# Second layer of a fused attention and two-layer kernel: the output product of two batches as seven block products in place of eight, with w_out streamed

## The chip, the cores and the metric

The kernel runs on one core of one Trainium2 chip. The metric is the time of one execution in device microseconds. TensorE (PE) does the matmuls, VectorE (DVE), ScalarE (ACT) and GpSimd (POOL) the rest, and SyncE's queue (SP) issues most DMAs.

## The reference

Everything is float32 in the result; the weights come as 64-bit floats.

```python
# attention: x (8, 8, 512, 64), state (8, 8, 32, 64)
attn_out = concat([xread, sread], axis=2)          # 512 + 32 rows per batch
x = attn_out.transpose(0, 2, 1, 3).reshape(4352, 512)
x = ((x @ w1) * (x @ w2)) @ w3 @ w_out             # first layer, d_ff 1024
out = ((x @ wa) * (x @ wb)) @ wo2                  # second layer, d_ff 1536
```

The change concerns the last line: `h = (x @ wa) * (x @ wb)`, of 1536 columns, times `wo2`, 1536 x 512. `wo2` is called w_out here where no other is meant.

## The kernel before

Each float32 operand of a matmul is split into a high and a low fp32r part, and three products (high-high, high-low, low-high; `PASSES`) are added up in PSUM. SBUF is managed by hand as 47 tiles ("units") of 128 x 1024 words; a unit is taken and given back in program order, with an estimated time at which it is free. All instructions of a queue run in program order. The code also keeps an estimate of the time on each engine, by which small tasks are put between the matmuls.

The first layer takes 0 to 565 us. While it runs, the weights of the second layer come in: class `Intake` ("ab") loads a block f of 128 columns of wa and wb as 64-bit words, converts them (ACT, DVE, POOL), makes the sums S1 to S4 of the quarter blocks A11 to A22, splits all of it, and stores it to DRAM (`w_d`). As a "third" it also converts the 128 rows f of w_out, splits them and stores them to `z_d`. Blocks 0, 1, 2, 9, 10, 11 (`AB_AT`) do so in the first layer, blocks 3 to 8 (`AB_LATER`) while pair 0 of the second layer runs; these stay in SBUF until used.

The second layer runs over four pairs g of batches (`block2`), the two batches being the columns of one 2 x 2 block product. For each of the 12 blocks f, the two products x @ wa and x @ wb of both batches come as seven block products (Winograd's form, `product`, L1497) of 6 matmuls of 512 columns, which accumulate in three PSUM banks r, v and q; ACT and DVE combine them into e1, e2, e5 and from these the h block of batch 2g (e1, cast and split at once) and that of batch 2g+1 (product of e2 and e5 on POOL, kept in f32 as hb). The output product of batch 2g is put between the products of the next f (`accumulate`, L1509): 4 tiles of 128 rows x 3 passes, 12 matmuls of 512 columns. After the last f, the h blocks of batch 2g+1 are split one by one (`second_split`) and multiplied, 144 matmuls, together with the last 12 of batch 2g. All 12 blocks of split w_out stay in SBUF (z_t). The weights `w_d` are loaded two blocks ahead, four units per f, and the features of the next pair (class `Features`, tiles xB and x) are loaded, subtracted and split in the output stage.

The 256 rows of the states are done once in pair 0: `state_step` for each f (24 matmuls of 256 columns, L1552) and `state_output` (72 of 512 columns, L1581).

```python
for c, (m, q) in enumerate(PASSES):           # output(), L1507
    nc.tensor.matmul(t, lhsT=h[:, m, part * P : (part + 1) * P], rhs=z_t[f][:, q, :], ...)
```

Of the kernel before, what the change touches and what calls it, by code (L numbers as in the profile page):

```python
# [43 lines left out]
SPLIT_AHEAD = 2  # L44
# [6 lines left out]
START_BY = 3.0  # L51
# [8 lines left out]
def attention_moe_moe2(  # L60
# [142 lines left out]
    z_d = [dp.tile([P, 2, DM], F32R, name=f"z_d{f}") for f in range(NF2)]  # L203
    w_d = [dp.tile([P, 4, 1024], F32R, name=f"w_d{f}") for f in range(NF2)]
# [690 lines left out]
    class Intake:  # L895
# [3 lines left out]
        def __init__(self, name, pair, third, order):  # L899
            self.name, self.pair, self.third, self.order = name, pair, third, order  # L900
            self.count = len(order)
            self.next = 0
            self.tasks = []
            self.cols = {}
            self.rows = {}

        def start(self, tasks=2, reserve=0):
            if (
# [8 lines left out]
                if self.third is not None:  # L917
                    raws.append(load64(f"{self.name}t{f}_", self.third[f * P : (f + 1) * P, :]))
                    t = charge(D=1.45) + 2.0
# [3 lines left out]
        def stages(self, f, raws):  # L923
# [10 lines left out]
            def take_third():  # L934
                o["t"] = Convert(f"{name}t", raws[2:])
                o["t"].take(0)

# [9 lines left out]
            def sums():  # L947
                a21, a22, a11, a12 = (halves(o["c"].out)[:, i] for i in range(4))
# [18 lines left out]
            def store_part(i):  # L967
                for j, t in enumerate(o["p", i]):
                    nc.sync.dma_start(out=w_d[f][:, 2 * i + j].bitcast(F32), in_=t.bitcast(F32))
                if f in AB_AT:  # L970
                    free(*(f"w0_{f}_{2 * i + j}" for j in range(2)), at=until[0] + 2.5)
                else:
                    w_t.setdefault((0, f), []).extend(
                        t.rearrange("p (b k c) -> p b k c", b=4, k=2) for t in o["p", i]
                    )
                self.cols[f] = i == 1

            def split_third():
                z = o["z"] = flat(unit(f"z{f}", F32R), DM)
                split(z[:, 0, :], z[:, 1, :], o["t"].out)  # L980
                free(f"{name}t")

            def store_third():
                nc.sync.dma_start(out=z_d[f].bitcast(F32), in_=o["z"].bitcast(F32))
                if f in AB_AT:
                    free(f"z{f}", at=until[0] + 2.5)
                else:
                    z_t[f] = o["z"]
                self.rows[f] = True
# [6 lines left out]
            if self.third is None:  # L996
                out.append((2, {"A": 1.1, eng: {"G": 2.4, "V": 1.1}[eng]}, split_columns))
            else:
# [3 lines left out]
                    (0, dict(A=1.1), take_third),  # L1002
                    (1, {eng: {"G": 2.6, "V": 1.4}[eng]}, sums),
                    (2, work, lambda: split_part(0)),
                    (1, dict(V=0.6, G=1.2), lambda: o["t"].make()),
                    (0, dict(D=3.0), lambda: store_part(0)),
                    (2, work, lambda: split_part(1)),
                    (1, dict(A=0.6, V=0.6), split_third),
                    (0, dict(D=3.0), lambda: store_part(1)),
                    (0, dict(D=1.5), store_third),  # L1010
# [20 lines left out]
        def need(self, f):  # L1031
            while f in self.order and (
                not self.cols.get(f) or self.third is not None and f not in self.rows
            ):
                left = len(vacant), len(self.tasks), sum(len(t[1]) for t in self.tasks)
                self.start()
                self.run(0, force=True)
                if left == (len(vacant), len(self.tasks), sum(len(t[1]) for t in self.tasks)):
# [3 lines left out]
    z_t = {}  # L1042
    sw = Intake("sw", (w1, w2), None, list(range(NF1)))
    ab = Intake("ab", (wb, wa), wo2, [*AB_AT, *AB_LATER])
# [109 lines left out]
    A21, A22, A11, A12, S1, S2, S3, S4 = range(8)  # L1154
    NG = B // 2

    def load_w(g, f):
# [3 lines left out]
        ts = []  # L1161
        for i in range(4):
            t = unit(f"w{g}_{f}_{i}", F32R)
            nc.sync.dma_start(out=t.bitcast(F32), in_=w_d[f][:, i].bitcast(F32))
            ts.append(t.rearrange("p (b k c) -> p b k c", b=4, k=2))
        w_t[g, f] = ts

    def load_z(f):
        if f in AB_LATER:
            return  # L1170
        z_t[f] = flat(unit(f"z{f}", F32R), DM)
        nc.sync.dma_start(out=z_t[f].bitcast(F32), in_=z_d[f].bitcast(F32))

    def weights(g, f, block, k):
        return [w_t[g, f][2 * (block // 4) + m][:, block % 4, k, :] for m in range(2)]
# [225 lines left out]
    for b in range(B):  # L1401
# [9 lines left out]
        def fills1(f, b=b):  # L1411
            def middle():
                attend(MIDDLE, b, f)
                sw.run(HORIZON[0])
                ab.run(HORIZON[0])

            def behind():
# [20 lines left out]
                if NF1 * b + f >= SW_FROM:  # L1438
                    sw.start(SW_TASKS, reserve=1)
                if NF1 * b + f >= AB_AT.get(ab.order[min(ab.next, NF2 - 1)], NF1 * B):  # L1440
                    ab.start(2, reserve=AB_RESERVE)
                sw.run(HORIZON[0])
                ab.run(HORIZON[0])

# [17 lines left out]
    def fills_s(f):  # L1462
        def middle():
            sw.run(HORIZON[1])
            ab.run(HORIZON[1])
            if f > 0:
                xf[0].run(1, keep=8 if sw.next < NF1 else 4)

        def behind():
# [5 lines left out]
            ab.run(HORIZON[1])  # L1475
            xf[0].run(1, keep=8 if sw.next < NF1 else 4)
            if f >= NF1 - 3 and (0, 0) not in w_t and room(5):
# [29 lines left out]
    def output(t, h, f, part, first, last):  # L1507
        for c, (m, q) in enumerate(PASSES):
            nc.tensor.matmul(  # L1509
                t,  # L1510
                lhsT=h[:, m, part * P : (part + 1) * P],
                rhs=z_t[f][:, q, :],
                start=first and c == 0,
                stop=last and c == 2,
            )
        now[0] += 3 * 512 / 2400 * 1.0625

# [6 lines left out]
    def store(i, t, o, nxt):  # L1524
        dst = out[i * SB : i * SB + S, :].rearrange("(p t) e -> p t e", t=NT)
        if nxt:
            if t % 2:
# [255 lines left out]
```

## Time and profile before

| what | us |
|---|---|
| median of 3 runs (lowest, highest) | 1343.9 (1341.16, 1345.19) |
| the profiled execution | 1342.51 |
| its span, first to last instruction | 1340.7 |
| PE busy | 1300.3 |
| DVE, ACT, POOL busy | 612.0, 550.2, 439.3 |
| mean granted TensorE clock | 0.988 |

The span is what the trace covers; the execution takes 1.8 us more. Matmuls overlap in the trace, so the sum of their durations is larger than the time in which PE is busy.

### The profile page before, as it was taken

How to read it: one execution, taken by the hardware profiler on the slowest of the kernel's cores; microseconds unless marked ns; L12 is line 12 of the kernel's file. 1: busy time of each engine (PE TensorE's matmuls, PEld its weight loads, DVE VectorE, ACT ScalarE, POOL GpSimd, SP SyncE). 2: the span in 40 equal slices, each digit the busy share in tenths (PEclk: the TensorE clock that was granted, in tenths of full speed). 3: DMA queues.
4: the chain of work that ended last, by engine and by line, in shares of the span. 5: the costliest groups of instructions: out<-in, count | busy, mean ns of one | idle time of the engine just before them, and what ended most of it. 6: DMA issues, size and time to landing. Idle time of an engine off the chain costs nothing.

```text
span 1340.7 us, 17395 instructions
## 1 busy us (share of the span) xinstructions
PE 1300.3 (97%) x6596; PEld 1054.2 (79%) x6596; DVE 612.0 (46%) x792; ACT 550.2 (41%) x951; POOL 439.3 (33%) x352
## 2 busy tenths in 40 slices
PE   3998999999999999999999999999999999999998
PEld 1765768778777789888888888888888888888876
DVE  6676215646666667455532712232722326323240
ACT  7676455655565666354421412211422114221130
POOL 5554214454464477255510430110411103211100
PEclk6999999999999999999999999999999999999999
DMA  9977368493566552777373265542664434744301
GB/s 312 285 234 236 110 205 246 140 290 126 205 205 219 173 174 74 241 269 264 126 267 110 95 215 193 173 149 72 222 218 158 150 115 149 246 173 157 110 0 64
DMA packets 120662, 240.24 MB, mean 179 GB/s; under 512 B 44673, under 2 KB 65153, under 8 KB 120577
## 3 DMA queue, kind: packets, MB, share of 16 engines
q1 hardware_dynamic: 116000, 222.86, 50.5%
q0 software_dynamic: 4576, 16.26, 3.1%
q8 instruction: 52, 0.85, 0.2%
q14 instruction: 34, 0.27, 0.1%
HBM read 173.54 MB, written 65.54 MB: 178 GB/s over the span
## 4 chain that ended last, share of the span: by engine, by line
PE 89%; DMA 4%; DVE 3%; ACT 2%; issue 1%; POOL 1%; SPq 1%; ACTq 0%; POOLq 0%; DVEq 0%
PE r L1497 20%; PE o L1509 19%; PE v L1497 10%; PE x2p L1110 9%; PE bp L1051 5%; PE q L1497 5%; PE ap L1051 5%; PE abs L1552 3%; PE wp L358 2%; PE pb L315 2%; PE x2f L1291 2%; PE f L1051 1%; PE os L1581 1%; PE xt L388 1%; PE bs L1051 1%
## 5 line engine op out<-in xcount | busy, mean ns | idle before, releaser
L1509 PE MATMUL o<-z,h 128*128 128x512 f32 x1152 | 276.6, 389 | 1.3 <-ACT h L136 1.3
L1509 PEld LDWEIGHTS o<-z,h 128*128 128x128 f32 x1152 | 216.1, 188 | 47.0 <-ACT h L136 1.7
L1672 POOL TENSOR_TENSOR hb<-e,e 128x512 f32<-128x512 f32 x48 | 62.9, 1311 | 453.5 <-DVE e L1522 453.4
L136 ACT CAST h<-e 128x512 fp32r<-128x512 f32 x48 | 29.8, 621 | 364.8 <-DVE e L1675 350.8
L1110 PE MATMUL x2p<-hp,ws 128*128 128x512 f32 x672 | 161.9, 390 | 0.0
L1110 PEld LDWEIGHTS x2p<-hp,ws 128*128 128x128 f32 x672 | 125.8, 188 | 26.2
L142 POOL TENSOR_TENSOR pl<-pr,ph 128x512 fp32r<-128x512 f32 x64 | 83.1, 1320 | 120.6 <-ACT ph L136 74.0
L1522 DVE TENSOR_TENSOR e<-e,q 128x512 f32<-128x512 f32 x48 | 33.0, 688 | 195.7 <-PE q L1497 195.7
L1075 DVE TENSOR_TENSOR hfp<-asbp,bp 128x512 f32<-128x512 f32 x56 | 38.3, 684 | 93.6 <-PE bp L1051 89.9
L142 DVE TENSOR_TENSOR hp<-hfp,hp 128x512 fp32r<-128x512 f32 x56 | 54.1, 965 | 40.0 <-ACT hp L136 38.7
L1522 DVE TENSOR_TENSOR e<-e,v 128x512 f32<-128x512 f32 x48 | 33.0, 688 | 85.4 <-PE v L1497 85.4
L1497 PE MATMUL r<-xT2h,w 128*128 128x512 f32 x192 | 67.1, 390 | 0.0
L1497 PE MATMUL r<-xB11h,w 128*128 128x512 f32 x192 | 66.9, 389 | 0.0
L1497 PE MATMUL v<-xT1h,w 128*128 128x512 f32 x192 | 66.9, 389 | 0.0
L1497 PE MATMUL q<-xB21h,w 128*128 128x512 f32 x192 | 66.9, 389 | 0.0
L1497 PE MATMUL r<-xT3h,w 128*128 128x512 f32 x192 | 66.9, 389 | 0.0
L1497 PE MATMUL v<-xB22h,w 128*128 128x512 f32 x192 | 66.9, 389 | 0.0
L1497 PE MATMUL r<-xT4h,w 128*128 128x512 f32 x192 | 66.9, 389 | 0.0
L136 ACT CAST hp<-hfp 128x512 fp32r<-128x512 f32 x56 | 34.7, 620 | 57.0 <-DVE hfp L1075 52.2
L1069 ACT COPY asbp<-ap 128x512 f32<-128x512 f32 x56 | 33.1, 591 | 56.3 <-PE ap L1051 56.2
L142 DVE TENSOR_TENSOR h<-e,h 128x512 fp32r<-128x512 f32 x48 | 35.5, 739 | 33.4 <-ACT h L136 33.4
L1051 PE MATMUL bp<-ah,ph 128*128 128x512 f32 x112 | 47.9, 428 | 1.4 <-DVE a L473 0.9
(476 smaller groups left out, 2815.4 us busy)
## 6 DMA issues: line engine op xcount, KB each, us to landing
w<-w_d SPq DMA_DIRECT2D x168, 512.0 KB, 5.1
w_d<-w SPq DMA_DIRECT2D x48, 512.0 KB, 2.9
p_d<-sg SPq DMA_DIRECT2D x128, 128.0 KB, 2.5
pr<-p_d SPq DMA_DIRECT2D x32, 512.0 KB, 5.2
x<-in_x_dram SPq DMA_DIRECT2D x64, 128.0 KB, 4.6
sw<-in_moe_w_dram SPq DMA_DIRECT2D x16, 512.0 KB, 5.2
xB<-x_d SPq DMA_DIRECT2D x16, 512.0 KB, 4.8
x_d<-x2sp POOLq DMA_DIRECT2D x14, 512.0 KB, 5.8
```

The costliest lines, as they stand in the source:

```text
L136: nc.scalar.copy(hi, src)
L142: (eng or nc.vector).tensor_tensor(out=lo[:, i], in0=src[:, i], in1=hi[:, i].bitcast(F32), op=ALU.subtract)
L315: nc.tensor.matmul(t, lhsT=st_s[rows, (bg * NP + p) * P : (bg * NP + p + 1) * P], rhs=conv[f"wk{p}_{nh}"].out[rows, half[i]], start=True, ...
L1051: nc.tensor.matmul(dst[:, :n], lhsT=l[m], rhs=r[q], start=i == 0 and j == 0, stop=i == k - 1 and j == 2,)
L1069: nc.scalar.copy(a_sb[:, :n], pa[:, :n])
L1075: nc.vector.tensor_tensor(out=hf[:, :n], in0=a_sb[:, :n], in1=pb[:, :n], op=ALU.mult)
L1110: nc.tensor.matmul(acc[j], lhsT=w_s[f][:, m, j * P : (j + 1) * P], rhs=h[:, q, :n], start=per == 1 and f == 0 and i == 0, stop=f == NF1 - ...
L1497: nc.tensor.matmul(t, lhsT=w[m], rhs=xf[g].parts[x][q][:, k, :], start=first and k == 0 and i == 0, stop=k == 1 and i == 2, skip_group_che ...
L1509: nc.tensor.matmul(t, lhsT=h[:, m, part * P : (part + 1) * P], rhs=z_t[f][:, q, :], start=first and c == 0, stop=last and c == 2,)
L1522: nc.vector.tensor_tensor(out=out, in0=x, in1=y, op=ALU.add)
L1552: nc.tensor.matmul(t[:, w * 256 : (w + 1) * 256], lhsT=l[m], rhs=x_s[k][q], start=k == 0 and i == 0, stop=k == 3 and i == 2,)
L1672: nc.gpsimd.tensor_tensor(out=h2[-1][:, f % 2, :], in0=e2, in1=e5, op=ALU.mult)
```

## The change

Both batches of a pair are now the two columns of a second block product. The h blocks of both are kept in f32 for the whole pair: the rows of h in two halves (f under 6 and from 6 on) and two batches make the blocks 11, 12, 21, 22, each of three chunks (j) of 1024 columns (two f of 512). POOL makes the sums S1 to S4 of h, each chunk one operation. w_out's halves are combined likewise: class `IntakeZ` converts rows c and c+6 together, makes T1 to T4 and stores the seven split operands to `z_d[p]`. Six such tasks are started at set steps of the first layer (`Z_AT`) or, if they are late, in pair 0.

The output stage has 21 steps (7 products p, 3 chunks j). A step has 24 matmuls of 256 columns: 2 blocks, 4 tiles of 128 rows, 3 passes. The h operand is split three steps ahead, and the w_out operand (512 KB) is loaded from DRAM three steps ahead, for each pair anew; no part of w_out stays in SBUF. Results are copied or added to the output tiles from the banks after each product. The last pair does its last product in two halves of the rows. The states' rows go the same way, 18 matmuls of 256 columns after each product of pair 0. In the loop over f no output matmul remains; T4 of f is issued after the first two products of f+1; weight units are reloaded one by one as they come free, in a new order of blocks (`PLACES`), 3.5 units per f for pairs 1 to 3; a block of weights is stored by eight DMAs of 256 KB in place of four of 512 KB.

```diff
-SPLIT_AHEAD = 2
+Z_AT = {0: 17, 1: 23, 2: 29, 3: 35, 4: 41, 5: 44}
+LOOK = 3
+Z_LOOK = 3
+PLACES = (0, 2, 6, 7, 1, 3, 4, 5)
+TERMS = ("11", "12", "S2", "S1", "S3", "S4", "22")
+X_FROM = 7
+W_AT = {11: 0, 17: 1}
...
-    z_d = [dp.tile([P, 2, DM], F32R, name=f"z_d{f}") for f in range(NF2)]
-    w_d = [dp.tile([P, 4, 1024], F32R, name=f"w_d{f}") for f in range(NF2)]
+    z_d = [dp.tile([P, NF2 // 2, 2, DM // 2], F32R, name=f"z_d{p}") for p in range(7)]
+    w_d = [dp.tile([P, 8, 2, 256], F32R, name=f"w_d{f}") for f in range(NF2)]
...
-                    nc.sync.dma_start(out=w_d[f][:, 2 * i + j].bitcast(F32), in_=t.bitcast(F32))
+                    for n in range(2):
+                        a, b = PLACES[4 * i + 2 * n : 4 * i + 2 * n + 2]
+                        nc.sync.dma_start(
+                            out=w_d[f][:, a : b + 1 : b - a, j, :].bitcast(F32),
+                            in_=t.rearrange("p (h b c) -> p h b c", h=2, b=2)[:, n].bitcast(F32),
+                        )
...
+    class IntakeZ(Intake):
...
+            def sums():
+                b11, b12, b21, b22 = (o["c"].out[:, i * 256 : (i + 1) * 256] for i in range(4))
+                o["s"] = unit(f"zs{c}")
+                t2, t1, t3, t4 = (o["s"][:, i * 256 : (i + 1) * 256] for i in range(4))
+                for out, x, y in ((t1, b12, b11), (t2, b22, t1), (t3, b22, b12), (t4, b21, t2)):
+                    nc.vector.tensor_tensor(out=out, in0=x, in1=y, op=ALU.subtract)
...
+    class Output:
...
+        def combine(self, out, x, y, op, eng="G"):
+            ENGINES[eng].tensor_tensor(out=out, in0=x, in1=y, op=op)
...
+        def split(self, p, j):
+            term = TERMS[p]
+            names = [f"r{self.name}_{term}{q}{j}" for q in "hl"]
+            hi, lo = (unit(n, F32R)[:, : self.width] for n in names)
+            name, src = self.raw[term, j]
+            split(hi, lo, src)
...
+    def z_load(g, p, j):
+        name = f"zz{g}_{p}_{j}"
+        t = unit(name, F32R).rearrange("p (c q e) -> p c q e", c=2, q=2)
+        nc.sync.dma_start(out=t.bitcast(F32), in_=z_d[p][:, 2 * j : 2 * j + 2].bitcast(F32))
...
+    CHAIN = "rqrvrvr"
+    FIRST = (True, True, False, True, False, False, False)
...
-            if one is not None:
-                accumulate(one, f - 1, (0, 1))
...
+            h = [flat(out2.raw[f"{i + 1}{half}", j][1], S)[:, c, :] for i in range(2)]
+            nc.gpsimd.tensor_tensor(out=h[1], in0=e2, in1=e5, op=ALU.mult)
+            if f + 1 < NF2:
+                begin(f + 1)
             product(r, g, f, A22, "T4", False)
-            nc.vector.tensor_tensor(out=e1, in0=e1, in1=r, op=ALU.mult)
-            one = flat(unit(f"h{name}", F32R), S)
-            split(one[:, 0, :], one[:, 1, :], e1)
+            nc.vector.tensor_tensor(out=h[0], in0=e1, in1=r, op=ALU.mult)
+            reload(f, 3)
...
+            if half == 2 and c == 1:
+                out2.split(0, j)
+                out2.sum("S1", j)
+                out2.sum("S3", j)
...
+        for s, (p, j, tiles) in enumerate(steps):
+            n = s + LOOK
+            if n < 21:
+                out2.split(*order[n])
+            if s == 0:
+                out2.sum("S2", 2)
+            if 5 <= s < 8:
+                out2.sum("S4", s - 5)
+            if s + Z_LOOK < 21:
+                z_load(g, *order[s + Z_LOOK])
+            if not last_pair:
+                if s in W_AT:
+                    load_w(g + 1, W_AT[s])
+                if s >= X_FROM:
+                    xf[g + 1].run(2 if s % 2 else 1)
...
+            for k in range(2):
+                for i in tiles:
+                    dst = banks[c, i // 2][:, i % 2 * 256 : i % 2 * 256 + 256]
+                    for n, (m, q) in enumerate(PASSES):
+                        nc.tensor.matmul(
+                            dst,
+                            lhsT=hl[m][:, k, i * P : (i + 1) * P],
+                            rhs=z[:, k, q, :],
...
+            if j == 2:
+                if g == 0:
+                    state_part(p)
+                evacuate(p, sorted({i // 2 for i in tiles}))
```

## Rows read from the trace of the kernel before

**Rows 1.** The page: busy time by engine; the chain that ended last, by engine.

```profile
PE 1300.3 (97%) x6596; PEld 1054.2 (79%) x6596; DVE 612.0 (46%) x792; ACT 550.2 (41%) x951; POOL 439.3 (33%) x352
...
PE 89%; DMA 4%; DVE 3%; ACT 2%; issue 1%; POOL 1%; SPq 1%; ACTq 0%; POOLq 0%; DVEq 0%
```

**Rows 2.** Waits of PE, whole span: us in total, times, longest.

```profile
PE w3t L344 <- POOL w L182: 22.3, 6, 14.3
...
PE o L1509 <- ACT h L136: 1.3, 1, 1.3
```

**Rows 3.** Windows: length; busy PE, PEld, DVE, ACT, POOL (instructions); PE clock, DMA share, GB/s.

```profile
190.00:480.00 290.00, 286.32 (x1774) 228.17 (x1773) 178.16 (x222) 169.82 (x300) 143.74 (x119) 1.00 0.64 204
...
565.00:743.00 178.00, 177.77 (x917) 152.40 (x916) 76.88 (x115) 65.28 (x113) 62.48 (x52) 1.00 0.59 210
...
939.00:974.00 35.00, 35.00 (x156) 29.01 (x155) 24.70 (x23) 15.49 (x23) 13.96 (x9) 1.00 0.68 235
```

**Rows 4.** Chain in order of time: start, us, engine, tile, line, instructions.

```profile
579.19 2.87 PE abs L1552 x24
...
743.01 35.36 PE o L1509 x156
778.37 16.32 PE os L1581 x72
```

**Rows 5.** Groups by form of ACT, DVE, POOL: busy us, mean ns, idle before.

```profile
L136 ACT CAST h<-e 128x512 fp32r<-128x512 f32 x48 | 29.8, 621 | 364.8 <-DVE e L1675 350.8 <-POOL hb L1672 14.0
...
L167 ACT ACTIVATE ab<-ab 128x512 f32<-128x512 f32 x24 | 16.1, 671 | 0.0
...
L275 ACT COPY ot<-o 128x512 f32<-128x512 f32 x16 | 9.2, 590 | 37.2 <-PE o L1509 37.2
...
L1563 ACT COPY as<-abs 128x256 f32<-128x256 f32 x12 | 4.5, 373 | 18.3 <-PE abs L1552 18.3
...
L136 ACT CAST xB11h<-xB 128x1024 fp32r<-128x1024 f32 x4 | 4.2, 1051 | 0.0
...
L176 DVE TENSOR_SCALAR ab<-ab 128x512 uint32<-128x512 uint32 x24 | 13.3, 592 | 2.9 <-ACT ab L167 2.9
L277 DVE COPY ot<-o 128x512 f32<-128x512 f32 x16 | 11.0, 690 | 40.6 <-PE o L1509 40.6
...
L142 DVE TENSOR_TENSOR xT1l<-xB,xT1h 128x1024 fp32r<-128x1024 f32 x4 | 4.9, 1220 | 0.0
...
L1564 DVE TENSOR_TENSOR hs<-as,abs 128x256 f32<-128x256 f32 x12 | 5.1, 422 | 29.7 <-ACT as L1563 29.7
...
L1672 POOL TENSOR_TENSOR hb<-e,e 128x512 f32<-128x512 f32 x48 | 62.9, 1311 | 453.5 <-DVE e L1522 453.4
L182 POOL TENSOR_TENSOR ab<-ab,ab 128x512 int32<-128x512 int32 x24 | 32.4, 1369 | 30.2 <-DVE ab L176 27.1 <-ACT ab L170 2.0 <-issue 1.0
```

**Rows 6.** DMA issues: queue, count, KB each, median us from issue to landing.

```profile
w<-w_d SPq DMA_DIRECT2D x168, 512.0 KB, 5.1
...
out_dram<-ot POOLq DMA_DIRECT2D x14, 512.0 KB, 4.7
...
out_dram<-ot SPq DMA_DIRECT2D x4, 256.0 KB, 2.7
```

**Rows 7.** Groups by form in 939 to 974 us, the output stage of pair 1.

```profile
L1217 POOL TENSOR_TENSOR xB<-xB,xB 128x1024 f32<-128x1024 f32 x2 | 6.1, 3052 | 4.3 <-issue 4.3
...
L142 DVE TENSOR_TENSOR xT3l<-xB,xT3h 128x1024 fp32r<-128x1024 f32 x1 | 2.3, 2306 | 0.0
...
L142 DVE TENSOR_TENSOR xT4l<-xB,xT4h 128x1024 fp32r<-128x1024 f32 x1 | 1.2, 1226 | 0.6 <-ACT xT4h L136 0.6
```

**Rows 8.** SP's timeline in pair 0: raw loads, first and last of four.

```profile
586.22 0.67 SPq L890 DMA_DIRECT2D ab<-in_moe_w_b_dram  x1
...
646.70 0.39 SPq L890 DMA_DIRECT2D ab<-in_moe_w_b_dram  x1
```

**Rows 9.** DVE's timeline: the last split of weight block 8.

```profile
675.89 1.23 DVE L142 TENSOR_TENSOR w<-ab8s,w 128x1024 fp32r<-128x1024 f32 x1 [2.13 <-ACT w L136]
```

More of the change, by code (lines that the diff above doesn't have):

```diff
@@ L947, in sums @@
             def sums():
-                a21, a22, a11, a12 = (halves(o["c"].out)[:, i] for i in range(4))
+                a11, a12, a21, a22 = (halves(o["c"].out)[:, i] for i in range(4))
                 o["s"] = unit(f"{name}s")
@@ L1031, in need @@
         def need(self, f):
[L1032 to L1035, printed above, removed]
+            while f in self.order and not self.cols.get(f):
+                left = self.next, len(vacant), len(self.tasks), sum(len(t[1]) for t in self.tasks)
                 self.start()
                 self.run(0, force=True)
-                if left == (len(vacant), len(self.tasks), sum(len(t[1]) for t in self.tasks)):
+                if left == (self.next, len(vacant), len(self.tasks), sum(len(t[1]) for t in self.tasks)):
@@ L1047, in mms @@
+    w_t = {}
+    iz = IntakeZ("z", None, False, list(range(NF2 // 2)))
     def mms(dst, n, pairs):
@@ L1505, in product @@
         now[0] += 6 * 512 / 2400 * 1.0625
[L1507 to L1516, printed above, removed]
     def temp(tag, name):
@@ new lines, in state_step @@
+        a_sb = hp.tile([P, 256], F32, tag="as", name=f"as2{f}", bufs=1)
+        nc.scalar.copy(a_sb, t[:, :256])
+        c = f % (NF2 // 2) * P
+        for i in range(2):
+            nc.vector.tensor_tensor(
+                out=hs[0].raw[f"{i + 1}{f // (NF2 // 2) + 1}", 0][1][:, c : c + P],
+                in0=a_sb[:, i * P : (i + 1) * P],
+                in1=t[:, 256 + i * P : 256 + (i + 1) * P],
+                op=ALU.mult,
+            )
+        charge(A=0.4, V=0.5)
+    CHAIN = "rqrvrvr"
@@ L1600, in block2 @@
+    FIRST = (True, True, False, True, False, False, False)
     def block2(g):
         last_pair = g == NG - 1
[L1602 to L1623 removed]
+        x = xf[g]
+        out2 = Output(f"{g}", 3, 1024)
+        steps = [(p, j, range(NT)) for p in range(7) for j in range(3)]
+        if last_pair:
+            steps[18:] = [(6, j, range(2 * b, 2 * b + 2)) for b in range(2) for j in range(3)]
@@ L1628, in more, with begin @@
                 ab.run(HORIZON[2])
-        for f in range(NF2):
+                if ab.next == ab.count:
+                    iz.start(1, reserve=Z_WAIT)
+                iz.run(HORIZON[2])
+        t = {}
+        def begin(f):
+            ab.need(f)
             name = f"{g}_{f}"
-            ab.need(f)
-            x = xf[g]
             r = bank(f"r{name}")
@@ L1645, in block2, with reload @@
             charge(A=0.6)
-            if g == 0:
-                more()
-                state_step(f)
+            t[f] = r, v, e1, e5
+            if f == NF2 - 1:
+                x.free("B11")
+                x.free("T1")
+        def reload(f, i):
+            if g:
+                free(f"w{g}_{f}_{i}")
+                if f + 2 < NF2:
+                    load_w(g, f + 2, [i])
+        begin(0)
+        if g == 0:
+            flush()
+        for f in range(NF2):
+            name = f"{g}_{f}"
+            half, j, c = f // (NF2 // 2) + 1, f % (NF2 // 2) // 2, f % 2
+            r, v, e1, e5 = t.pop(f)
+            reload(f, 0)
             product(r, g, f, S2, "T2", False)
```

407 lines of the change are left out of this document (233 added, 174 removed).

## The prediction, on record before the result

> **What bounds the kernel now.** The page comes first: TensorE is busy for 97% of the span and holds 89% of the chain that ended last [rows 1]. Next the waits by who waited: PE's longest wait, 22.3 us in total, is for a conversion near the start; in the second layer there is one of 1.3 us, for an ACT cast at the end of the last pair [rows 2]. The windows say the same by stage: PE is busy in 177.8 of 178 us of pair 0's loop and in 35 of 35 of an output stage at full clock, with DVE, ACT and POOL below half in the first of them [rows 3]. So in the second layer time is what PE's instruction stream takes; other engines and DMA count only if they come late. The chain in order of time gives the price of that stream [rows 4]: 156 matmuls of 512 columns in 35.36 us are 226.7 ns each, 24 of 256 columns (each with its own weight load, as in the new code) in 2.87 us are 119.6 ns each. The durations of single matmuls overlap and are no price.
>
> **Output products.** Removed: 1152 matmuls of 512 columns, 1152 x 0.2267 = 261.1 us. Added: 7 products x 3 chunks x 2 blocks x 4 tiles x 3 passes = 504 matmuls of 256 columns per pair, 2016 in all, x 0.1196 = 241.1 us. Seven for eight would be 32.6 us off if a column cost the same; but the two prices fit a share per column plus 2 x 119.6 - 226.7 = 12.5 ns for each matmul whatever its width, and the number of matmuls rises by 75%. Gain: 20.0 us (5.0 a pair). The state rows' product goes from 72 wide ones, 16.32 us [rows 4], to 7 x 6 x 3 = 126 narrow ones, 15.07 us: 1.25 us.
>
> The Trainium skill, "TensorE: Matmul & The Clock Gate", section "Back-to-back issue gap", gives N/2.4 + 2.5 ns for a warm matmul: 215.8 and 109.2 ns. The trace does not agree (226.7 and 119.6). By the page's figures the gain would be 7.1 us a pair and 2.0 for the state, an estimate of 30 us in place of 21.
>
> **The wait at the end of the last pair.** In the kernel before, the last h block is multiplied, cast and only then used (1.27 us idle). The new first product takes block 11, whose rows are complete at f = 5 and whose chunks are split from f = 7 on. This goes: 1.3 us. Gains so far 22.5 us.
>
> **The loop over f.** Per f, PE loses the 12 output matmuls in it (12 x 0.2267 = 2.72 us): it takes 42 x 0.2267 = 9.52 us, and 12.4 with the state step of pair 0 (15.1 before). T4 comes after the next f's first two products, so each PSUM bank is read by ACT or DVE while PE does 2.72 us of other products; the reads take 0.59 and 0.69 us [rows 5]. ACT has three copies per f (1.8 us), DVE four operations (2.8), POOL one (1.3); the state step, moved behind T4, feeds only sums that are used in the output stage. Cost nothing, and without this cover under 1 us per f. Weights for f+2 are 3.5 loads of 0.524 MB in 9.52 us, 193 GB/s; the stage 939 to 974 moved 235 GB/s at a DMA share of 0.68 [rows 3], so some 345 GB/s full. Nothing.
>
> **The output stage of a pair**, 21 steps of 24 narrow matmuls, 2.87 us each, 60.3 us in all. By the means of such operations [rows 5], DVE has 18 splits plus 7 operations for the next pair's features at 1.22 us and 10 bank reads at 0.69: 37 us. ACT: 25 casts at 1.05 and 4 copies at 0.59: 29 us. POOL: about 6 sums of 1024 columns and 4 feature operations, each at two of its 512-wide ones (2 x 1.31): 26 us. All under 60. Each split is issued 3 steps (8.6 us) before its use, each bank has a whole product (8.6 us) between its last matmul and the next writer. Taken: nothing; bounds below, in the rivals.
>
> **Streamed w_out.** One load of 0.524 MB per step, asked 3 steps ahead; loads of this size landed in 5.1 us [rows 6]. 183 GB/s alone. On SP's in-order queue, four feature loads go in between steps 7 and 9 and the next pair's weights at step 11: steps 7 to 12 ask for 13.5 x 0.524 = 7.1 MB in 17.2 us, 411 GB/s against 345, which ends 3.3 us late; the slack is 8.6 - 5.1 = 3.5 us. Taken: 0; upper bound 3.3 us for three pairs, 10 us.
>
> **Where pair 0 ends.** With two extra banks for the state rows all eight are handed round, so the next pair's first product takes the bank of the last output tile. Its ACT read stands behind the state copy (0.37 us), which waits for the last state matmul: 0.37 + 0.59 + two handovers, about 1.3 us of PE idle. Bounds 0 and 2.
>
> **First layer.** Six tasks that convert w_out (and sums and splits of 1792 columns each) move wholly into it; half of the old thirds were there. A task, by the means of such operations [rows 5]: ACT four activations at 0.67, three casts at 0.62 and one at 0.41, 5.0 us; DVE two shifts at 0.59, four sums at 0.42, three low parts at 0.69 and one at 0.42, 5.4 us; POOL two additions at 1.37, 2.7 us. Six tasks are 30, 33 and 16 us. An old third cost ACT 2.0, DVE 1.3 and POOL 1.4; the six that stood there leave with 12, 8 and 8. So the stretch 190 to 480 gains about 18 us of ACT, 25 of DVE and 8 of POOL. DVE was busy 178 of 290 us there and PE idle 3.7 [rows 3]; by proportion 25/178 x 3.7 = 0.5 us. From below 0, from above all 25; I take 1.5, near the proportion, since each hidden product is used one step late.
>
> **The tail.** The last store is 512 KB in place of 256 KB: 4.7 us for the one, 2.7 for the other [rows 6], after a copy of 0.69 us as before: 2.0 us more. Bounds 0 and 2.5.
>
> Sum: 22.5 - 1.3 - 1.5 - 2.0 = 17.7 us. The profiled execution took 1342.5 us (span 1340.7, 1.8 around it), so 1324.8; the median of the runs shown is 1.4 above it: **1326.2 us**.
>
> **Rivals.**
> *DVE and POOL hold each other up.* Beside POOL, a DVE operation of 1024 columns took 2.31 us in place of 1.23, and POOL's own 3.05 [rows 7]. If all 25 of a stage cost 2.25, DVE needs 56 + 7 = 63 us against PE's 60.3: 2.9 us in each of three pairs and nearly all slack gone: 8.7 us, about 1335. For it: twelve sums of 1024 columns per pair are new on POOL. Against: POOL has 26 us of work in 60, so not all can collide. The Trainium skill, "SBUF — State Buffer", section "Who interferes with whom", says that a DVE instruction with two SBUF inputs contends with a GpSimd one that reads SBUF, one blocking the other; by that rule the time would be this rival's, and the slow split agrees with it. 0.14.
>
> *The stream is late.* The 3.3 us above in three pairs: 10 us, 1336. For it: the sum of what steps 7 to 12 ask; against: SP issues when a tile is free, not when PE reaches the step, so it runs ahead. 0.13.
>
> *Pair 0's weights are late (the other side).* Blocks 3 to 8 are converted while pair 0 runs. The raw loads of blocks 5 to 8 went out between 586.2 and 646.7 us, 20 us apart on average [rows 8], and the last split of block 8 ended at 677.1 [rows 9]; its use was at 565 + 8 x 15.1 = 686. Now f = 8 begins at 565 + 8 x 12.4 = 664. At the old pace PE waits 13 us here and the time is 1339, the edge of no change. If the task is later than before, which stores in twice as many and smaller pieces on the same SP queue can cause, each us is lost: from 5 us later, 682, the gain is gone; at 10 us later 23 us are lost, 1349. Against: the code starts a task when enough tiles are vacant, and 12 tiles of w_out no longer stay. 0.08 for the old pace, 0.07 for later.
>
> *The change doesn't do what it says*: narrow matmuls at another price. At the price of a column in wide ones (113.4 ns) 13 us more come off, 1313; the state steps speak against it. (By the Trainium skill's figures above it would be 1317, an estimate.) 0.05.
>
> **How the numbers follow.** Forecast 0.53 (its own range 1320 to 1331). The range 1319 to 1341 leaves out the last rival (0.05), the later weights (0.07) and some of the edges. Within 0.3% (4 us, about what these runs tell from none) lies the old pace: same 0.08; slower 0.07; the rest is faster, 0.85.
>
> **What would show it.** 2016 + 126 narrow matmuls, 24 in 2.87 us; the gap between two pairs' first products 114.2 + 60.3 = 174.6 us in place of 179.5; PE waits of about 1 us where pair 0 ends and none on the streamed tile; DVE some 37 of 60 us in an output stage. Wrong if PE waits in each output stage for an ACT or DVE split or for a load, or before f = 4 to 8 of pair 0 for a weight tile, or if the first layer ends past 566 us.

## The result and the profile after

The changed kernel takes 1330.8 us (median of four runs) beside 1343.5 for the kernel before on the same chip. One of the four was disturbed (1824.83 us at a mean clock of 0.652); the other three lie between 1328.25 and 1332.53 us with 1329.2 in the middle, and the ratio, 0.990 with an interval of 0.987 to 0.993, is theirs. The change is faster, by about 1%: 12.7 us by the medians, 14.4 with the middle one of the three. The forecast was 1326.2 and 17.7 us of gain. A second series on another chip gave 1331.5 and a ratio of 0.992 (0.991 to 0.993).

The page of the changed kernel, its busy line, the chain by engine and the lines of the new transfers, answers to [rows 1] and [rows 6]:

```profile
PE 1285.2 (97%) x7514; PEld 1082.9 (81%) x7514; DVE 744.7 (56%) x861; ACT 584.9 (44%) x958; POOL 579.7 (44%) x396
...
PE 81%; DVE 2%; ACT 2%; DMA 2%; issue 1%; POOL 1%; SPq 0%; POOLq 0%; ACTq 0%
...
w<-w_d SPq DMA_DIRECT2D x132, 512.0 KB, 7.8
zz<-z_d SPq DMA_DIRECT2D x84, 512.0 KB, 4.4
```

PE still fills 97% of a shorter span, with 918 more matmuls; DVE has 133 us more work and POOL 140, and neither has a larger share of the chain than before. To see where the time went, the span is cut at the first product of each pair. Windows of the changed kernel (start and end, length, then busy time of PE, PEld, DVE, ACT and POOL, PE clock, DMA share, GB/s):

```profile
563.44:798.80 235.36, 229.77 (x1437) 206.96 (x1436) 150.17 (x187) 99.32 (x154) 126.57 (x80) 0.99 0.71 240
798.80:974.60 175.80, 175.02 (x1010) 154.98 (x1009) 91.85 (x85) 51.14 (x70) 66.06 (x38) 1.00 0.59 212
974.60:1150.42 175.82, 175.04 (x1011) 155.03 (x1010) 92.51 (x86) 50.45 (x69) 64.01 (x34) 1.00 0.59 213
1150.42:1330.80 180.38, 175.19 (x1010) 154.97 (x1008) 80.19 (x80) 43.57 (x62) 49.84 (x26) 1.00 0.49 178
```

Beside the same cuts in the trace of before, and the terms of the forecast put into their stretches:

| stretch, us | before | after | change | forecast |
|---|---|---|---|---|
| up to pair 0's first product | 561.1 | 563.4 | +2.3 | +1.5 |
| pair 0 | 233.4 | 235.4 | +1.9 | -4.9 |
| pair 1, pair 2, each | 179.5 | 175.8 | -3.7 | -5.0 |
| pair 3, to the end of the span | 187.1 | 180.4 | -6.8 | -4.3 |
| span | 1340.7 | 1330.8 | -9.9 | -17.7 |

The row "up to pair 0's first product" is mostly spread between runs. The new tasks run after the first matmul into the tile x2p, at about 190 us. From there to pair 0's first product it is 372.0 to 372.1 us in five profiles with this first layer (this one and experiments 6, 7, 9 and 11), beside 371.3 before: 0.7 us more. What lies ahead of that point takes 188.3 to 192.9 us in the same profiles, 191.4 in this one and 189.8 before.

The later pairs gain, pair 0 loses. PE idles 0.78 us in each of pairs 1 and 2 (length less busy) and 5.6 in pair 0. Who waits, in the waits of PE (us in total, times, longest), which answer to [rows 2]:

```profile
PE r L1557 <- DVE e L1571: 4.1, 5, 1.0
...
PE r L1557 <- ACT e L1719: 2.0, 2, 1.8
PE ro L1875 <- DMA zz<-z_d: 1.7, 1, 1.7
```

Four of the five waits of the first row are at the end of a pair's loop over f, the fifth (the longest) is early in pair 0. For pair 1, the chain in order of time (start, us, engine, tile, line, matmuls):

```profile
911.90 0.70 DVE e L1571
912.60 0.04 issue
912.64 1.66 PE r L1557 x6
914.30 8.62 PE ro L1875 x72
922.93 8.64 PE qo L1875 x72
```

T4 of the last f needs bank r, from which DVE still has to add e5. In every other f two products of f+1 stand between; here none is left, so PE waits out the read. Behind it, 72 narrow matmuls take 8.62 to 8.64 us, up to 120.0 ns each, beside 119.6 in [rows 4].

The other two waits are in pair 0. Timeline there (start, us, engine, line, operation; in brackets the idle time before it and its releaser), from SP's, ACT's and PE's rows:

```profile
673.47 0.89 SPq L158 DMA_DIRECT2D zr<-in_moe_w_out_dram  x2
...
682.50 0.66 ACT L174 ACTIVATE zr<-zr 128x512 f32<-128x512 f32 x1 [4.18 <-DMA zr<-in_moe_w_out_dram]
...
686.86 0.62 ACT L143 CAST za<-z 128x512 fp32r<-128x512 f32 x1 [1.60 <-POOL z L189]
687.38 0.58 ACT L1719 COPY e<-r 128x512 f32<-128x512 f32 x1
...
688.01 0.50 PE L1557 MATMUL r<-xT3h,w 128*128 128x512 f32 x1 [1.79 <-ACT e L1719]
```

The raw rows of w_out's last task (L158) went out at 673 and landed at 682; ACT, in order, stood 4.2 us before converting them, then 1.6 us before the cast of the result, which waits for POOL, and the copy of e2 for the product of this f stood behind that. So a conversion of w_out, meant for the first layer, holds up PE in pair 0. It costs more than the 1.79 us, as the windows show:

```profile
684.00:688.00 4.00, 2.23 (x10) 1.50 (x8) 1.82 (x4) 2.35 (x5) 2.40 (x2) 1.00 0.64 260
688.00:690.00 2.00, 1.99 (x8) 1.63 (x9) 1.95 (x6) 0.98 (x3) 0.00 (x0) 0.88 0.49 184
690.00:692.00 2.00, 2.00 (x6) 1.56 (x5) 2.00 (x5) 0.47 (x1) 0.00 (x0) 0.50 0.62 229
692.00:694.00 2.00, 2.00 (x8) 1.60 (x7) 1.10 (x2) 0.59 (x1) 1.42 (x1) 0.76 0.68 254
694.00:696.00 2.00, 2.00 (x14) 1.74 (x13) 0.58 (x1) 0.59 (x1) 0.25 (x1) 1.00 1.02 301
```

After the idle time the granted clock fell to 0.50, that is 1.2 GHz for 2.4, for 3.4 us, and about 1.7 us more were lost. PE counts as busy in these rows: a slow clock is not seen in the busy share, only in the clock column and in the number of instructions.

In the output stage of pair 1, by windows, then DVE's and POOL's groups by form (count, busy us, mean ns), which answer to [rows 3] and [rows 7]:

```profile
914.00:975.00 61.00, 61.00 (x508) 60.91 (x507) 53.45 (x37) 24.46 (x27) 33.24 (x15) 1.00 0.75 264
```

```profile
L149 DVE TENSOR_TENSOR r_12l<-r,r_12h 128x1024 fp32r<-128x1024 f32 x3 | 10.1, 3429 | 0.0
L149 DVE TENSOR_TENSOR r_S2l<-r,r_S2h 128x1024 fp32r<-128x1024 f32 x3 | 7.3, 2485 | 0.0
...
L149 DVE TENSOR_TENSOR r_S1l<-r_S,r_S1h 128x1024 fp32r<-128x1024 f32 x3 | 3.5, 1211 | 0.0
```

DVE is busy 53 us for the 37 forecast: a split of the same size takes 1.21 us at one place and 3.43 at another. Yet PE is busy in 61 of 61 us.

### The profile page after: what moved, and what is told of

Its sections match the earlier page's. It is cut to its first block, busy times and chain, and to the rows that moved or that the text cites. A ratio compares the mean times of both kernels' runs of the same rounds, so it can differ in the third digit from the quotient of the medians.

```text
span 1330.8 us, 19755 instructions
## 1 busy us (share of the span) xinstructions
PE 1285.2 (97%) x7514; PEld 1082.9 (81%) x7514; DVE 744.7 (56%) x861; ACT 584.9 (44%) x958; POOL 579.7 (44%) x396
## 2 busy tenths in 40 slices
DMA packets 155134, 276.56 MB, mean 208 GB/s; under 512 B 47136, under 2 KB 92192, under 8 KB 155040
## 4 chain that ended last, share of the span: by engine, by line
PE 81%; DVE 2%; ACT 2%; DMA 2%; issue 1%; POOL 1%; SPq 0%; POOLq 0%; ACTq 0%
PE r L1557 19%; PE ro L1875 10%; PE x2p L1167 10%; PE v L1557 9%; PE vo L1875 5%; PE bp L1108 5%; PE ap L1108 5%; PE q L1557 5%; PE qo L1875 3%; PE abs L1640 2%; PE x2f L1345 2%; PE pb L322 1%; PE srv L1814 1%; PE bs L1108 1%; PE f L1108 1%
## 5 line engine op out<-in xcount | busy, mean ns | idle before, releaser
L1740 POOL TENSOR_TENSOR r<-e,e 128x512 f32<-128x512 f32 x48 | 63.5, 1322 | 284.2 <-DVE e L1571 284.2
L1691 ACT COPY e<-r 128x512 f32<-128x512 f32 x48 | 28.2, 588 | 190.0 <-PE r L1557 189.9
L1746 DVE TENSOR_TENSOR r<-e,r 128x512 f32<-128x512 f32 x48 | 33.0, 687 | 134.3 <-PE r L1557 134.3
L1595 POOL TENSOR_TENSOR r<-r,r 128x1024 f32<-128x1024 f32 x24 | 71.8, 3007 | 0.9
L1719 ACT COPY e<-r 128x512 f32<-128x512 f32 x48 | 28.2, 587 | 70.8 <-PE r L1557 70.8
L1557 PEld LDWEIGHTS r<-xT4h,w 128*128 128x128 f32 x192 | 36.0, 188 | 14.0 <-DVE e L1571 6.6
```

What stands on the lines that cost most here:

```text
L1557: nc.tensor.matmul(t, lhsT=w[m], rhs=xf[g].parts[x][q][:, k, :], start=first and k == 0 and i == 0, stop=k == 1 and i == 2, skip_group_che ...
L1595: ENGINES[eng].tensor_tensor(out=out, in0=x, in1=y, op=op)
L1740: nc.gpsimd.tensor_tensor(out=h[1], in0=e2, in1=e5, op=ALU.mult)
L1746: nc.vector.tensor_tensor(out=h[0], in0=e1, in1=r, op=ALU.mult)
```

## The experiments

The theory: the arithmetic of the products is as forecast; what is missing lies in the last f of each pair (T4 without cover) and in pair 0, where w_out is converted late. The rivals: the tasks come too early rather than too late; the contention of DVE and POOL, or the streamed w_out, is paid after all; narrow matmuls cost more than their columns. The letters A, B, C are those of each expectation. Experiments 1 to 4, 5 to 8, and 9 and 10 ran side by side, 11 alone. Each ratio is to the kernel before, timed beside the experiment; these medians of the kernel before differ by up to 1.9 us, so ratios compare better than times.

**1. Cover for the last T4.** The first output step (in pair 0 the last state step) goes between the last f's S3 and T4.

```diff
             if f + 1 < NF2:
                 begin(f + 1)
+            elif g == 0:
+                state_step(f)
+            else:
+                for pj in order[:Z_LOOK]:
+                    z_load(g, *pj)
+                out_step(0)
...
```

> The changed kernel, with work of PE put between S3 and T4 of the last f of a pair: the first output step in pairs 1 to 3, the state step of f = 11 in pair 0. Theory A (part of the gain that is missing is four waits of 0.8 us at T4, because the last f has no next products to cover DVE's add): the wait of r for DVE's add falls from 4.1 us to about 1 (one in the middle of pair 0 stays), a pair takes 175.0 us in place of 175.8, and the time is 3 us under the changed kernel's. Theory B (the output stage runs behind DVE anyway, which is busy 88% of it): the 0.8 us come back as a wait for a split in the first steps, and the time stays.

1327.4 us, ratio 0.988 (0.986 to 0.989). Its chain in order of time:

```profile
911.48 1.36 PE r L1557 x6
912.84 2.87 PE ro L1745 x24
915.71 1.39 PE r L1557 x6
917.10 5.75 PE ro L1745 x48
```

No wait stands before T4 any more; the wait for DVE's e falls from 4.1 us in five places to 0.9 in one. Pairs 1 and 2 take 174.76 us for 175.81: 1.05 us a pair, the forecast length of 174.6 but for 0.2. Pair 0 gains nothing in the profiled run (236.3 us; the clock fell there twice). Theory A holds for pairs 1 to 3; for pair 0 see experiment 9.

**2. All tasks of pair 0 four microseconds later.** If ACT stands before raw rows that have not landed, tasks that start later would spare the wait.

```diff
-                self.tasks.append([t + MARGIN, self.stages(f, raws)])
+                self.tasks.append([t + MARGIN + late[0], self.stages(f, raws)])
...
+        late[0] = 4.0
```

> The changed kernel, with every conversion task that is started from the second layer on treated as ready 4 us later, so that its ACT operations stand further behind in ACT's queue. Theory A (in pair 0 ACT stands waiting for raw rows of w_out that land late, 4.2 us once, and the copy of e2 behind it makes PE wait 1.8 us and then run 3.4 us at half clock): that wait and the clock's fall go, and the time is 3 to 4 us under the changed kernel's. Theory B (pair 0 has too little time for its conversions, wherever they stand): the wait moves to another operation or to the weights of a later f, and the time stays or grows.

1361.4 us, ratio 1.013 (1.012 to 1.015). Pair 0 takes 264.4 us; PE waits 23.1 us for the first w_out tile and 9.0 for DVE's e. Theory B: a shift of 4 us grows to 29. Why it grows (a later task finds no vacant tile) is argued here; experiment 6 shows one such place.

**3. The operands exchanged.** h becomes the moving operand (512 columns) and w_out the weights: 36 matmuls a product for 72. Output and additions are then turned (each 128 x 128 block transposed), so this one leaves out the turning back.

```diff
-                            lhsT=hl[m][:, k, i * P : (i + 1) * P],
-                            rhs=z[:, k, q, :],
+                            lhsT=z[:, k, q, i * P : (i + 1) * P],
+                            rhs=hl[m][:, k, :],
```

> The changed kernel, with the operands of the output product exchanged: w_out's columns are the weights and 512 rows of h move, so a pair has 252 matmuls of 512 columns in place of 504 of 256, the same columns in all; the blocks of the output are written transposed, so the output is not the reference's. Theory A (a matmul has a fixed share of some 13 ns whatever its width): 252 x 0.2267 = 57.1 us in place of 60.5 a pair, 13 us under the changed kernel's time. Theory B (the price goes by columns, and the gain was lost elsewhere): no change. Theory C (DVE at 88% of the stage is the next bound): PE waits for splits, and 3 to 6 us of the 13 are lost.

1322.2 us, ratio 0.985 (0.983 to 0.986). Its chain in order of time, and two of PE's waits:

```profile
739.50 8.19 PE ro L1875 x36
747.69 2.15 PE srv L1814 x18
```

```profile
PE vo L1875 <- DMA zz<-z_d: 2.5, 1, 2.5
...
PE ro L1875 <- DVE r_22l L149: 1.3, 2, 0.6
```

A wide matmul is 227.5 ns here, so 36 take 0.45 us less than 72 narrow ones: the price of narrow ones is a price for each matmul, not for its columns. Of the 3.2 us a pair that seven products would give, 2.4 arrive (173.37 for 175.81); the shorter stage begins to wait for a split, and the last pair for a tile.

**4. The sums of h on DVE.** Takes POOL's sums away, and with them what runs beside DVE's splits.

```diff
-        def combine(self, out, x, y, op, eng="G"):
+        def combine(self, out, x, y, op, eng="V"):
```

> The changed kernel, with the twelve sums of h a pair (and the states') on DVE in place of POOL. Theory A (DVE and POOL hold each other up, but behind PE's cover): splits of 1024 columns fall from 2.2 to 3.4 us to about 1.2, DVE's busy time in an output stage stays near 45 to 55 of 61 us, the time stays within 2 us. Theory B (the mutual hold-up costs time): the time falls by several us. Theory C (DVE has no room for 15 us more in the last f's): PE waits for DVE at the end of a pair, slower by 2 to 6 us.

1332.4 us, ratio 0.992 (0.990 to 0.993): no change against the changed kernel. Windows and DVE's groups by form in the output stage of pair 1:

```profile
912.00:973.00 61.00, 61.00 (x508) 60.92 (x507) 48.76 (x43) 24.57 (x27) 14.21 (x9) 1.00 0.77 264
```

```profile
L149 DVE TENSOR_TENSOR r_12l<-r,r_12h 128x1024 fp32r<-128x1024 f32 x3 | 3.6, 1219 | 0.0
```

This split falls from 3.43 to 1.22 us without POOL's sums beside it, and the pair stays at 175.81: theory A. Three groups of splits (12, S2, 11) give 11.7 of the 16 us by which DVE was over the forecast; those of S4 stay at 2.21, so POOL's sums are not the whole of it. The contention is real and costs nothing in these pairs, where each split has three steps (8.6 us) of lead. In pair 0 it does cost something once PE no longer waits for a tile there (experiments 7 and 9).

**5. Half of w_out is not converted.** Rows 3 to 5 and 9 to 11 are left out; the sums of the other rows stand in their place.

```diff
+                    for r in (c, c + 3):
+                        nc.sync.dma_start(out=z_d[p][:, r].bitcast(F32), in_=v[:, i].bitcast(F32))
...
-    iz = IntakeZ("z", None, False, list(range(NF2 // 2)))
+    iz = IntakeZ("z", None, False, list(range(3)))
```

> The changed kernel, with w_out's row blocks 3 to 5 (and 9 to 11) not converted at all: those of 0 to 2 are stored in their place, so half of w_out is left out of the result. The three conversion tasks that ran inside pair 0 are gone, the w_out operand's loads and all matmuls stay. Theory A (pair 0, 235.4 us long where 227 were to be had, pays for these tasks by waits of PE and a fall of its clock): pair 0 takes 228 to 231 us, and the time is 5 us under the changed kernel's. Theory B (pair 0 pays for the conversion of weight blocks 3 to 8, which has less time than before): pair 0 stays at 233 or more.

1328.0 us, ratio 0.989 (0.987 to 0.991). In the loop of pair 0 each f from the fifth on takes 12.42 us, the forecast (from one T2 product to the next), where two of them took 12.67 and 16.14 after the change: 4.0 us. The output stage starts 3.6 us sooner after the pair's first product. Then PE waits 3.1 us for a w_out tile (1.7 after the change), and the clock falls again. Windows around it:

```profile
720.00:724.00 4.00, 0.94 (x5) 0.73 (x5) 4.00 (x3) 3.04 (x4) 3.92 (x2) 0.81 1.00 406
724.00:728.00 4.00, 4.00 (x21) 4.00 (x20) 4.00 (x2) 0.00 (x0) 4.00 (x3) 0.50 0.38 156
728.00:732.00 4.00, 4.00 (x31) 4.00 (x31) 4.00 (x3) 0.00 (x0) 4.00 (x2) 0.84 0.45 131
```

Pair 0 takes as long as it did (235.8 us) in the profiled run, the slowest of the four (1327.2 to 1332.3): theory B's figure, though not by its mechanism alone. The late tasks cost 4.0 us in the loop of the changed kernel's profile, and what their absence frees is lost again at the first tiles, which are asked for only when the output stage is reached. Part of the 4.0 us is the fall of the clock: in the profiles of experiments 7, 8, 9 and 11, where it did not fall at that place, the same two f cost 2.3 to 2.8 us. The wait for the tile is not the late tasks' doing, since it is longer without them.

**6. The w_out tasks alone 2.5 us later.**

```diff
-                self.tasks.append([charge(D=2.9) + 2.0 + MARGIN, self.stages(c, raws)])
+                self.tasks.append([charge(D=2.9) + 2.0 + MARGIN + late[0], self.stages(c, raws)])
...
+        late[0] = 2.5
```

> The changed kernel, with only the w_out tasks of pair 0 treated as ready 2.5 us later (the weight tasks stay). Theory A (the copy of e2 stands behind activations on raw rows that land late): the wait of r for ACT's copy falls from 1.8 us to under 0.5, the clock stays up, the tasks still end before the output stage, and pair 0 takes about 232 us. Theory B (the room in time is gone, as with 4 us for all tasks): the wait for the first w_out tiles grows from 1.7 us to 5 or more, pair 0 takes 236 us or more.

1356.3 us, ratio 1.009 (1.007 to 1.012). One of PE's waits, and the last raw loads in SP's timeline:

```profile
PE ro L1878 <- DMA zz<-z_d: 23.8, 1, 23.8
```

```profile
694.45 7.16 SPq L158 DMA_DIRECT2D zr<-in_moe_w_out_dram  x2
```

As in experiment 2 (theory B), pair 0 takes 258.1 us: the last raw rows went out only at 694.5 and 701.3 us, as SP waited 8.0 and 6.4 us before them for tiles that PE's matmuls had still to free, and the last of the products of w_out was stored at 735.

**7. The first tiles asked for one f sooner.** The last w_out task is finished and the first three tiles are loaded before the last f of pair 0.

```diff
+            if g == 0 and f == NF2 - 1:
+                for i in range(NF2 // 2):
+                    iz.need(i)
+                for i in range(Z_LOOK):
+                    z_load(g, 0, i)
...
```

> The changed kernel, with the first three w_out tiles of pair 0's output stage asked for at the start of f = 11 in place of after it. Theory A (they land late because they are asked late, at 716 us): the wait of 1.7 us at the second step goes, pair 0 is 1.7 us shorter. Theory B (the conversion's last stores stand ahead of them, or SP waits for a vacant tile): SP issues them no earlier, and the wait stays.

1328.2 us, ratio 0.988 (0.986 to 0.990). In PE's waits that for the tile is gone; a shorter one for a split stands in the same stage:

```profile
PE qo L1881 <- DVE r_12l L149: 0.6, 1, 0.6
```

Pair 0 takes 233.25 us, and no window of it shows a lower clock, though PE idled 1.70 us for the e2 copy at 684.5. Theory A, as far as the wait goes; of the 2.1 us that pair 0 is shorter, 1.2 are in the f of the e2 copy, where the clock did not fall this time.

**8. No stream.** Pairs 1 to 3 use the tiles of the first product for all seven, so six of seven loads are left out.

```diff
+        if g and p:
+            z_t[g, p, j] = z_t[g, 0, j]
+            return
...
```

> The changed kernel, with the w_out operand of the first product used for all seven in pairs 1 to 3: 18 of 21 loads of 512 KB a pair are left out, so the output is not the reference's. Theory A (the stream costs nothing in these pairs): a pair stays at 175.8 us and the share of the DMA engines in an output stage falls from 0.75 to about 0.35. Theory B (late tiles slow PE a little without a wait of their own): a pair falls below 175.5 us.

One run, 1332.4 us. The window of pair 1's output stage:

```profile
914.00:975.00 61.00, 61.00 (x508) 60.87 (x507) 53.55 (x37) 24.56 (x27) 33.28 (x15) 1.00 0.40 137
```

The DMA share falls from 0.75 to 0.40 and the pairs stay at 175.8 us. The stream costs nothing in these pairs (theory A).

**9. Experiments 1 and 7 together**, with both edits as shown.

> The changed kernel with the work put between S3 and T4 of a pair's last f and with the first three w_out tiles of pair 0 asked for at the start of its f = 11. Theory A (the two losses are separate waits and add up): a pair takes 174.8 us, pair 0 about 232 us with no fall of the clock behind the tile wait, and the time is 5 to 6 us under the changed kernel's. Theory B (with the waits at its end gone, pair 0 waits elsewhere: for ACT's copy of e2 or for a split): pair 0 stays above 234 us and the gain is 3 us.

1325.9 us, ratio 0.987 (0.986 to 0.989), beside 1331.5 and 0.992 for the changed kernel (experiment 11, on another chip). Pair 0 takes 233.15 us, pairs 1 and 2 174.76. What is left in PE's waits of the second layer:

```profile
PE r L1557 <- ACT e L1778: 1.9, 2, 1.7
...
PE qo L1745 <- DVE r_12l L149: 1.7, 1, 1.7
...
PE r L1557 <- DVE e L1571: 1.1, 2, 0.9
```

That is theory A's gain, and its pairs 1 to 3. In pair 0 the cover gave 0.1 us over experiment 7 (233.25): the wait for r_12's split grew from 0.6 to 1.7 us instead. DVE's splits there take 2.6 to 3.4 us, with POOL's sums beside them, so by the trace this is the contention of DVE and POOL, paid after all, and theory B's mechanism in small; no run with POOL's sums taken out of this version was made. 16.3 us under the kernel before, this has the lowest median of the versions that compute the whole, but its ratio is not clear of those of experiments 1 and 7 (0.988 each); that the two gains add up is shown by the traces, not by the times.

**10. Experiments 9 and 3, turned back.** DVE transposes 32 x 32 pieces of the output and the store puts them in place.

```diff
+        nc.vector.transpose(t, src)
...
+        for q in range(4):
+            c0 = e * 256 + b * P + 32 * q
+            eng.dma_start(
+                out=rows[:, :, :, c0 : c0 + 32],
```

> The same kernel with w_out's columns as weights and 512 rows of h moving (252 wide matmuls a pair in place of 504 narrow ones), and the transposed output blocks turned back: DVE transposes 32 x 32 squares of each finished half tile, and POOL's queue stores them in pieces of 128 bytes. Theory A (the matmul count sets PE's part, DVE and DMA have the room): a pair takes 171.5 to 172.5 us, the tail grows by 1 to 3 us, the time is 8 to 11 us under that of the kernel with narrow matmuls. Theory B (DVE, busy 88% of an output stage before, gets 5 us more and PE waits for splits; or small pieces delay the tiles of w_out): 3 us a pair are lost to waits and the gain is under 3 us.

1358.3 us, ratio 1.012 (1.010 to 1.014). Four of PE's waits, and one of ACT's in the output stage of pair 1:

```profile
PE vo L1765 <- DMA zz<-z_d: 8.7, 1, 8.7
PE ro L1765 <- ACT r_22h L143: 8.5, 3, 2.9
PE vo L1765 <- DVE r_S4l L149: 4.7, 4, 1.3
PE ro L1765 <- DVE r_22l L149: 3.3, 5, 0.8
```

```profile
ACT xT4h L143 <- POOL xB L1271: 11.9, 1, 11.9
```

Theory B, by more than it foresaw. Pairs 1 and 2 take 181.5 us for 174.8, with waits in the output stage that were not there, and packets under 512 B rise from 47136 to 65312. In pair 1, 3.3 us of these waits are for DVE's splits, with the transposes between them, and 2.9 for a cast of ACT: it stands behind the cast of a feature tile, which waits 11.9 us for POOL, and POOL issues the small stores before it computes that tile. The last pair takes 194.9 us for 179.3; 11.1 us of the difference are two waits for w_out tiles (8.7 and 2.4), whose loads stand behind eight small stores each on SP's queue (5.3 to 5.5 us of issuing). What the wide form gives (2.4 us a pair) doesn't pay for turning it in this way.

**11. The changed kernel again**, as it is, for comparison with experiments 9 and 10.

> The changed kernel as it is, timed again beside the kernel before. If its shortfall against the forecast is the waits seen in its trace (four of 0.8 us at T4, some 6 us in pair 0 with a fall of the clock), the time lies at 1328 to 1331 us and its pairs 1 and 2 take 175.8 us again; if the first profile was an unlucky one, pair 0 takes 230 us or less here.

1331.5 us (1328.88 to 1333.55), ratio 0.992 (0.991 to 0.993); pair 0 237.1 us, pairs 1 and 2 175.8. So the shortfall is that of the waits, at 0.5 us past the range named for it, and the first profile was not an unlucky one. What differs between runs of it is pair 0 (here a wait of 3.3 us for a w_out tile, and a clock that fell behind it and not behind the e2 copy) and the start of pair 0 (560.6 us for 563.4).

## Why the prediction was right, and where its terms were off

The direction, the mechanism and the range held. The median lies 4.6 us above the forecast, 3.0 if 1329.2 is taken, 5.3 in the second series; in the profiled execution the span gained 9.9 us for 17.7.

- **Output products, 20.0 us.** The price was 120.0 ns for 119.6: 504 a pair are 60.5 us, the gain 4.8 a pair and 19.2 in all. That a narrow matmul costs more than its columns was shown by experiment 3. The formula of the Trainium skill, "TensorE: Matmul & The Clock Gate", section "Back-to-back issue gap", which that section gives for a matmul by itself, would make it 109.2 and the wide one 215.8, an estimate; neither is seen in any run here (120.0 and 226.7 to 227.5). By these figures the states' product would gain 1.8 us, not the 2.0 of the prediction.
- **The loop over f, "Cost nothing".** This step failed, for one f in twelve. The text argued from the cover that the next f gives and priced its loss ("under 1 us per f"), but did not ask which f has no next one. The last has none: 1.05 us a pair, which experiment 1 takes away in pairs 1 to 3. In pair 0 the same 1.05 us is in the trace, but the cover does not win it there (experiment 9).
- **The wait at the end of the last pair, 1.3 us.** It is gone, with no such row in PE's waits. It was worth 1.9: behind the wait of 1.43 in the trace of before, three more matmuls started 0.1 to 0.2 us late.
- **The first layer, "move wholly into it", 1.5 us.** This step failed, and with it pair 0. The stretch from 190 us to pair 0's first product grew by 0.7 us, near the proportion of 0.5, but with half of the work: three of the six tasks ran in pair 0, where the forecast put none. There they cost 4.0 us in the loop (experiment 5), clock included, and 2.3 to 2.8 where the clock did not fall. The loads of their raw rows show it: of twelve, from 228 to 674 us, half went out after 565. Why they came so late no run here shows; the code starts a task only where it counts six vacant tiles. The sign "past 566 us" was met in this profile, where the last matmul of the first layer starts at 567.5 (565.2 before), but the same code gives 564.5 to 569.0 in other profiles.
- **Streamed w_out, nothing.** Right in pairs 1 to 3 (experiment 8). In pair 0 the tile of the second output step came 1.7 us late (3.3 in experiment 11), and experiment 7 takes that wait away. The text priced steps 7 to 12, where SP issues most, and not the first tiles, which have no earlier step to be asked in.
- **Where pair 0 ends, 1.3 us.** Not paid: no idle time stands between pair 0's last output matmul and pair 1's first product. The bound of nothing was right.
- **The tail, 2.0 us.** Not paid; the end is shorter. Timeline of the last copy:

```profile
1326.42 0.69 DVE L1795 COPY ot<-ro 128x512 f32<-128x512 f32 x1 [7.95 <-PE ro L1875]
```

  The span ends 4.7 us after the start of the last matmul, in the trace of before 6.0. Two medians of DMA groups ([rows 6]) were set against each other, of which the larger was of another queue.
- **The output stage, nothing.** Right in the time. The size of DVE's work was not: 53 us for 37, of which POOL's sums account for some 12 (experiment 4). The Trainium skill, "SBUF — State Buffer", section "Who interferes with whom", says that a DVE instruction with two SBUF inputs contends with a GpSimd one that reads SBUF, and the durations agree (3.43 and 1.22 us); the time that the rival drew from it (1335) did not come, since the lead covers the slow splits in pairs 1 to 3. The stream rival (1336) falls with experiment 8. It also took 345 GB/s for full, while one window of experiment 5 moved 406.
- **Pair 0's weights late.** PE waits 0.2 us for a weight tile: the old pace did not hold. The side of pair 0 was right to fear, the weights were the wrong part of it.

Pair 0 by these: 6.9 us over its forecast, 8.2 if the 1.3 us not paid are counted. The starts of its matmuls say where: 4.0 for the late tasks, 1.8 at the tile, 1.05 at the last T4, and 2.3 in the second and third f, which take 12.86 and 14.28 us for 12.42. Half of the last is one wait, at T4 again. Timelines of DVE, then of PE:

```profile
602.08 0.68 DVE L1571 TENSOR_TENSOR e<-e,r 128x512 f32<-128x512 f32 x1
```

```profile
602.81 0.50 PE L1557 MATMUL r<-xT4h,w 128*128 128x512 f32 x1 [0.98 <-DVE e L1571]
```

From 595.4 to 600.6 us DVE was busy with the conversion of weight blocks, and its three adds for this f came behind it. Experiment 5 keeps these 2.3 us, so the three late tasks are not their cause; what would take them away was not tried. Against them stands 1.3 us that the kernel before lost, and the changed one does not, at its first state step, which now comes behind T4. Its row in the trace of before, where a later such step takes 2.87 us of the chain [rows 4]:

```profile
565.28 4.37 PE L1552 MATMUL abs<-xs,w 128*128 128x256 f32 x24
```

These add up to 7.9 of the 8.2 us.

Faster still was experiment 9, at the forecast: with T4 covered and the tiles asked for in time, 1325.9 us. That is agreement by errors that cancel, for pair 0 still has its late tasks, and the transition and the tail are cheaper than was put down.

## What to carry to other kernels

When a wait is hidden by the next step of a loop, price the last step by itself: it has no next one, and it comes once per outer loop. When work is moved into an earlier stage, read whether that stage can take it; otherwise it comes late, and on an engine that works in order it stands before work that the bottleneck needs. Slow work on an engine that is not the bottleneck costs nothing as long as its results have lead, and shows as soon as the lead is spent: the same splits of r_12 take 3.4 us without a wait in pair 1 and hold PE up by 1.7 us in pair 0 of experiment 9.

## What was not expected of the hardware

- An idle time of PE could cost about twice its length. After 1.8 us of waiting the granted clock was 0.50 (1.2 GHz) in 690 to 692, and lower than full for 3.4 us; after 3.1 us in experiment 5 for 6.8 us. In experiment 7 PE waited 1.70 us and the clock stayed at 1.00, and of two waits for the same tile one of 2.2 us (experiment 8) was followed by a fall and one of 2.3 us (experiment 4) was not. So the same wait is not always followed by a fall, and two runs of one kernel differ by it.
- A DVE split of 1024 columns took 1.21 to 3.43 us by what POOL did beside it, more than the 2.31 seen in [rows 7].
- The DMA engines moved 406 GB/s in a window of 4 us at a share of 1.00, and 345 GB/s at a share of 1.03 in another, between 588 and 601 us of the changed kernel.
